# Block means of the first batch's values: from vector reductions to products with a constant matrix

## The chip, the cores and the metric

The kernel runs on one core of a Trainium2 chip. Its engines have queues of their own, each in a fixed order: TensorE (PE, with its weight loads as PEld), VectorE (DVE), ScalarE (ACT), GpSimd (POOL), and SyncE (SP), which issues nearly all transfers. What is measured is the device time of one execution in microseconds (us); lower is better. Line numbers such as L349 are lines of the kernel before; where the changed kernel's own lines are meant, the text says so.

## The reference

Three stages follow each other: an attention, a feed-forward block h - tanh(h), and a gated feed-forward block with a norm in front.

```python
block, window = (32, 16)                     # B, H, S, D = 2, 8, 768, 64; nb = 24
k_sum = k.reshape(B, H, nb, block, D).max(axis=3)
v_sum = v.reshape(B, H, nb, block, D).mean(axis=3)
scores_l = scale * q @ k^T                   # kept only where |i - j| < 16
scores_s = scale * q @ k_sum^T + log(block)
a = softmax(concat(scores_l, scores_s))
x = a @ concat(v, v_sum)                     # 1536 tokens x 512
h = x @ w_in;  x = (h - tanh(h)) @ w_out     # 512 -> 2048 -> 512
xn = x / rms(x) * rms_g
out = (silu(xn @ w_gate) * (xn @ w_val)) @ w_out2
```

What the change touches is `v_sum` of batch 0 (24 blocks by 512 columns), and, lightly, `k_sum`.

## The kernel before, in words

**Attention.** A tile is 128 queries of one batch, 6 tiles a batch. A unit u is half the heads of one tile: u = 0 to 11 belong to batch 0, 12 to 23 to batch 1; the units of batch 0 are taken in the order 0, 2, 1, 3, 4, 5, ... For a unit, `scores` (L333) multiplies the queries with a window of keys beside the 24 block maxima on TensorE, four products of 120 columns (L346); VectorE adds the mask and finds the maximum (L349, four steps of two instructions); ScalarE takes the exponential (L351); VectorE finishes the sums (L352, L353); GpSimd scales (L354). `trans` (L357) turns the result on TensorE (L361) and copies it (L366), and `pv` (L369) multiplies it with the values (L378), after which ScalarE writes the high part of a tile's output x (L381) and VectorE its low part (L382). Three tiles make a group; the first product of the feed-forward block with group 0, `up_step` (L405, products L395 to L397), needs the x of units 0 to 5. "The third x" below is the one of units 4 and 5.

**Block maxima and means.** `ksum_a` (L248) loads one of two halves of a batch's keys for one parity of heads and reduces them on VectorE (L263 to L266); `ksum_b` (L268) turns them into a table (L272, L274 to L276). `vsum_a` (L278) loads a quarter of the values, laid out with a block's 32 rows side by side, and sums them: in batch 0 three quarters by a reduction on VectorE (L294), one by five additions on GpSimd (L290, L292). `vsum_b` (L296) turns the sums with four transposes (L300) and writes them, scaled, into a values tile (L304 on ScalarE, L306 on VectorE), from which a second tile gets them by two small transfers (L331).

**Weights.** Each of 16 + 16 weight tiles of the first block arrives as pairs of 32-bit words; ScalarE and VectorE make one float of each pair (L162 to L165), and ScalarE or VectorE and GpSimd split it into two parts (L170 or L172, L173). The first words of `w_in` are worked on while the attention of batch 0 runs.

**What sets the order.** `task` (L580) gives every piece of work a due time; pieces are emitted in that order, and a list scheduler with a time model of its own then lays the instructions of each engine into a fixed queue. An engine that stands at an instruction whose input is late stands still. `tc.issue_after(i)` ties what is emitted under it behind instruction i of the same engine. SP issues its transfers in order; at most eight are under way, since the ninth waits for the first.

Of the kernel before, what the change touches and what calls it, by code (L numbers as in the profile page):

```python
# [2 lines left out]

# [50 lines left out]
TP1 = 1.0  # L54
TC = 0.6
TK01 = 1
TV = 4
TK1 = -8
TV1 = -8
TD0 = 11  # L60
# [17 lines left out]
TVL = (6, 16)
ORD = [0, 2, 1, 3]
TKB = (4, 6)  # L80
VE = ((0, 1, 0, 0), (1, 1, 1, 1))
DTV = 0.25
TVS = 10
TCKW = {"schedule_with_timeline_sim": True}


# [1 line left out]
def attn_moe_kernel(ctx: ExitStack, tc: tile.TileContext, ins, out, dbg=None):  # L88
    nc = tc.nc
    V, A, G, T = nc.vector, nc.scalar, nc.gpsimd, nc.tensor  # L90

    cst = ctx.enter_context(tc.tile_pool(name="cst", bufs=1))
    wp = ctx.enter_context(tc.tile_pool(name="wp", bufs=SLOTS_A))
# [9 lines left out]
    ps_t = att_ctx.enter_context(tc.tile_pool(name="ps_t", bufs=PST, space=PSUM))  # L103
    ap1 = att_ctx.enter_context(tc.tile_pool(name="ap1", bufs=1))
# [6 lines left out]
    state = {}  # L111

    def f(ap):
        return ap.bitcast(F32)

    sel = cst.tile([128, 256], F32, name="sel")
    ident = sel[:, 64:192]
    rg = cst.tile([128, KD], F32, name="rg")
    mask = ap1.tile([128, 3, WID], F32, name="mask")


    def consts():
        nc.sync.dma_start(out=mask, in_=ins["mask"])
        nc.sync.dma_start(out=rg, in_=ins["rms_g"])


    jobs = []
# [120 lines left out]
    def ksum_a(b, par, hf):  # L248
        if not kwin:
            for h2 in range(2):  # L250
                for p2 in range(2):
                    kwin[0, p2, h2] = kp_.tile([128, KT, 4 * WID], F32, name="kw")
        if b:
            kwin[b, par, hf] = kp_.tile([128, KT, 4 * WID], F32, name="kw")
        kw = kwin[b, par, hf]
        m1 = ap2.tile([128, KT, 2, 4], F32, name="m1")
        m2 = ap2.tile([128, KT, 2, 4], F32, name="m2")
        if not hf:
            kmax[b, par] = ap2.tile([128, 4, TPB, 2], F32, name="mx")
        ts = slice(hf * KT, hf * KT + KT)  # L260
        nc.sync.dma_start(out=kw[:, :, 0:4 * LOC], in_=ins["kw"][b, par, :, ts])
        w = kw[:, :, 0:4 * LOC].rearrange("p t (j k c) -> p t j k c", j=4, k=4)
        V.tensor_reduce(m1.rearrange("p t j k -> p t (j k)"), kw[:, :, 96:288].rearrange("p t (x c) -> p t x c", c=24), AX.X, ALU.max)  # L263
        for j in range(2):
            V.tensor_reduce(m2[:, :, j], w[:, :, 3 * j, :, 16:24], AX.X, ALU.max)
        V.tensor_tensor(kmax[b, par][:, :, ts].rearrange("p k t j -> p t j k"), m1, m2, ALU.max)  # L266
# [11 lines left out]
    def vsum_a(b, c, pool, name):  # L278
# [3 lines left out]
        raw = pool.tile([128, 1024], U32, name=name) if name == "raw" else pool.tile([128, 2, 512], F32R, name=name).rearrange("p a n -> p (a n)")  # L282
        rr = f(raw)[:, 0:S]
        nc.sync.dma_start(out=rr, in_=ins["vt"][b, c])
        r = rr.rearrange("p (n j) -> p n j", j=BLK)
        o = vt_[b][:, c, LOC:]
        if VE[b][c]:
            n = BLK // 2
            while n > 1:
                G.tensor_tensor(r[:, :, 0:n], r[:, :, 0:n], r[:, :, n:2 * n], ALU.add)  # L290
                n //= 2
            G.tensor_tensor(o, r[:, :, 0], r[:, :, 1], ALU.add)  # L292
        else:
            V.tensor_reduce(o, r, AX.X, ALU.add)  # L294

    def vsum_b(b):  # L296
        vt = vt_.pop(b)
        ps = ps_t.tile([128, 512], F32, name="t")
        for c in range(4):
            T.transpose(ps[0:WID, c * 128:(c + 1) * 128], vt[:, c], ident)  # L300
        if b == 0:
            v_of[0] = 0
            vsum[b] = v_b[0][LOC:WID, 0]
            A.activation(v_b[0][LOC:WID, 0], ps[LOC:WID], AF.Copy, scale=1.0 / BLK)  # L304
            if PVS[b]:
                V.tensor_scalar(v_b[0][LOC:WID, 1], ps[LOC:WID], 1.0 / BLK, None, ALU.mult)  # L306
            else:
                A.activation(v_b[0][LOC:WID, 1], ps[LOC:WID], AF.Copy, scale=1.0 / BLK)
            return
        vsum[b] = ap1.tile([128, DM], F32, name="vsum")[LOC:WID]  # L310
        if PVS[b]:
            V.tensor_scalar(vsum[b], ps[LOC:WID], 1.0 / BLK, None, ALU.mult)
        else:
            A.activation(vsum[b], ps[LOC:WID], AF.Copy, scale=1.0 / BLK)
# [72 lines left out]
    for j, nch in enumerate(NCH):  # L387
# [4 lines left out]
    acc, part, gs, last = {}, {}, {}, {}  # L392
# [187 lines left out]
    def task(key, at, fn, *req):  # L580
        plan[key] = (at + SHIFT.get(key, 0), len(plan), fn, req)
# [14 lines left out]
    for par in range(2):  # L596
        at = TK01 * par
        for hf in range(2):
            task(f"ka0{par}{hf}", at + hf / 4, lambda par=par, hf=hf: ksum_a(0, par, hf))
        task(f"kb0{par}", TKB[par], lambda par=par: ksum_b(0, par), f"ka0{par}0", f"ka0{par}1", "sel")  # L600
    for c in range(4):
        task(f"va0{c}", TV + c * DTV, lambda c=c: vsum_a(0, c, wp, "w"))
    task("vs0", TV * 0 + TVS, lambda: vsum_b(0), "sel", *[f"va0{c}" for c in range(4)])
    at = t_sc(2 * TPB)
    for par in range(2):
        for hf in range(2):
            i = 2 * par + hf + 4 - KBUF
            task(f"ka1{par}{hf}", at + TK1 + 4 * par + 2 * hf, lambda par=par, hf=hf: ksum_a(1, par, hf), *([f"sc{[4, 5, 10, 11][i]}"] if i >= 0 else []))
        task(f"kb1{par}", at - 2 + par, lambda par=par: ksum_b(1, par), f"ka1{par}0", f"ka1{par}1")
    for c in range(4):  # L610
        task(f"va1{c}", at + TV1 + 3 * c, lambda c=c: vsum_a(1, c, rawp, "raw"))
# [18 lines left out]
    at = TM0  # L630
# [62 lines left out]
    for i in range(n0, len(steps) + LAG):  # L693
# [18 lines left out]
        j, g, m, first, end = steps[i - LAG]  # L712
# [5 lines left out]
        if j == len(NCH) - 1 and end:  # L718
            t = free["t"]
# [31 lines left out]
        down2(*prev, j)  # L751


_INS = ["q", "kw", "vt", "vw", "mask", "sel", "rms_g", "w_in", "w_out", "w_gate", "w_val", "w_out2"]


def layouts(q, k, v, moe_w_in, moe_w_out, moe2_w_gate, moe2_w_val, moe2_w_out, moe2_rms_g):
# [15 lines left out]
    vt = v.transpose(0, 2, 1, 3).reshape(B, S, DM)  # L773
# [17 lines left out]
    return {  # L791
        "q": qz.reshape(B, TPB, 128, 1024),
        "kw": np.ascontiguousarray(kw).reshape(B, 2, 128, TPB, 4 * LOC),
        "vt": np.ascontiguousarray(vs), "vw": np.ascontiguousarray(vw),
        "mask": mask,
        "sel": np.eye(128, dtype=np.float32).reshape(128, 2, 1, 64).repeat(2, axis=2).reshape(128, 256),
        "rms_g": np.ascontiguousarray(moe2_rms_g.reshape(KD, 128).T),
# [21 lines left out]
```

## Time and profile before

| | |
|---|---|
| median of 3 runs | 659.62 us (656.51, 659.62, 776.9) |
| profiled execution, its own time | 658.16 us |
| its span in the trace | 656.4 us |
| TensorE busy | 625.1 us (95%) |
| VectorE busy | 451.1 us (69%) |
| ScalarE, GpSimd busy | 324.6 us (49%), 227.7 us (35%) |
| share of TensorE in the chain that ended last | 86% (VectorE 9%) |

From about 82 us on TensorE is busy nearly all the time, but for some 8 us around 357 us and 360 to 380 us, between the two feed-forward blocks, and the last few. In the first 50 us it stands still for 18 us. The granted clock is read with care there: products of the same form take twice as long at 16 us as at 22 us, and the clock column shows 1.00 for both.

### The profile page before, as it was taken

The numbers are of one execution on the slowest core, as the hardware profiler recorded it, in microseconds if no ns is written. First come the engines' busy times: TensorE is split into PE (matmuls) and PEld (weight loads), VectorE is DVE, ScalarE is ACT, GpSimd is POOL, SyncE is SP. The second block draws the span as 40 slices with busy tenths as digits, with TensorE's granted clock in tenths as the row PEclk, the third lists the DMA queues.
The fourth block names the chain that finished last, engine by engine and source line by source line (L and its number), as shares of the span: only waits on it lengthen the run. The fifth ranks groups of instructions, "written<-read, shape, count | busy, mean of one in ns | idle before, by whom it ended". The sixth has DMA issues, their size and how long they took to land.

```text
span 656.4 us, 9788 instructions
## 1 busy us (share of the span) xinstructions
PE 625.1 (95%) x3576; PEld 571.3 (87%) x3576; DVE 451.1 (69%) x979; ACT 324.6 (49%) x783; POOL 227.7 (35%) x237
## 2 busy tenths in 40 slices
PE   3779999999999999999997799999999999999997
PEld 3768898899998999999996699999999999999995
DVE  5898654368887666756469476766768767678644
ACT  2776676445444444444556584454544554454320
POOL 1467621112322222440014020635634644555300
PEclk9888999999999999999999789999999999999999
DMA  9986321212322322111000000121121211111013
GB/s 335 353 280 205 120 93 43 89 65 97 128 97 86 107 93 101 65 65 65 0 33 32 33 1 0 65 82 47 65 91 38 96 66 64 65 66 64 1 49 144
DMA packets 19641, 58.91 MB, mean 90 GB/s; under 512 B 2169, under 2 KB 5497, under 8 KB 19593
## 3 DMA queue, kind: packets, MB, share of 16 engines
q1 hardware_dynamic: 19592, 58.29, 25.7%
q8 instruction: 28, 0.46, 0.3%
q14 instruction: 21, 0.16, 0.1%
HBM read 54.84 MB, written 3.15 MB: 88 GB/s over the span
## 4 chain that ended last, share of the span: by engine, by line
PE 86%; DVE 9%; ACT 2%; issue 1%; DMA 1%; POOL 0%; SPq 0%; DVEq 0%; ACTq 0%
PE h L395 8%; PE h L397 8%; PE h L396 8%; PE acc L401 6%; PE acc L402 6%; PE acc L403 6%; PE t L401 5%; PE t L402 5%; PE t L403 5%; PE acc L395 4%; PE acc L397 4%; PE acc L396 4%; PE accx L397 3%; PE accx L396 3%; PE accx L395 3%; PE t L346 2%
## 5 line engine op out<-in xcount | busy, mean ns | idle before, releaser
L173 POOL TENSOR_TENSOR w<-dt,w 128x512 fp32r<-128x512 f32 (+1 forms) x59 | 73.8, 1252 | 191.6 <-ACT w L170 139.8
L395 PE MATMUL h<-x,w 128*128 128x384 f32 x248 | 85.5, 345 | 7.5 <-DVE s L414 6.4
L397 PE MATMUL h<-x,w 128*128 128x384 f32 x248 | 84.7, 343 | 2.3 <-DVE x L382 2.3
L162 ACT ACTIVATE da<-raw 128x512 f32<-128x512 f32 x68 | 45.6, 670 | 81.5 <-DMA raw<-w_out 32.3
L396 PE MATMUL h<-x,w 128*128 128x384 f32 x248 | 84.6, 341 | 0.0
L414 DVE TENSOR_TENSOR s<-h,s 128x384 f32<-128x384 f32 x64 | 35.5, 555 | 46.5 <-ACT s L413 46.2
L417 DVE TENSOR_TENSOR g<-s,g 128x384 fp32r<-128x384 f32 x64 | 47.5, 743 | 22.4 <-ACT g L416 22.2
L395 PE MATMUL acc<-x,w 128*128 128x384 f32 x168 | 57.8, 344 | 0.0
L396 PE MATMUL acc<-x,w 128*128 128x384 f32 x168 | 57.3, 341 | 0.0
L402 PE MATMUL acc<-w,g 128*128 128x512 f32 x144 | 57.2, 397 | 0.0
L402 PE MATMUL t<-w,g 128*128 128x512 f32 x144 | 56.8, 395 | 0.0
L403 PE MATMUL t<-w,g 128*128 128x512 f32 x144 | 56.6, 393 | 0.0
L437 DVE TENSOR_TENSOR part<-t,part 128x512 f32<-128x512 f32 x60 | 40.5, 686 | 23.2 <-PE t L403 23.2
L395 PEld LDWEIGHTS h<-x,w 128*128 128x128 f32 x248 | 47.3, 191 | 10.5 <-DVE s L414 6.8
L403 PE MATMUL acc<-w,g 128*128 128x512 f32 x144 | 56.1, 397 | 0.0
L397 PE MATMUL acc<-x,w 128*128 128x384 f32 x168 | 55.7, 341 | 0.0
L401 PE MATMUL acc<-w,g 128*128 128x512 f32 x144 | 55.3, 400 | 0.0
L401 PE MATMUL t<-w,g 128*128 128x512 f32 x144 | 54.8, 394 | 0.3 <-DVE part L437 0.3
L164 DVE SCALAR_TENSOR_TENSOR dt<-da,dt 128x512 uint32<-128x512 uint32 x68 | 53.8, 791 | 1.6
L165 DVE SCALAR_TENSOR_TENSOR dt<-raw,dt 128x512 uint32<-128x512 uint32 x68 | 51.4, 756 | 1.3
L170 ACT ACTIVATE w<-dt 128x512 fp32r<-128x512 f32 (+1 forms) x55 | 32.0, 583 | 40.7 <-DVE dt L165 40.2
L413 ACT ACTIVATE s<-h 128x384 f32<-128x384 f32 x64 | 30.9, 483 | 41.2 <-PE h L397 41.0
(130 smaller groups left out, 1547.4 us busy)
## 6 DMA issues: line engine op xcount, KB each, us to landing
raw<-w_out SPq DMA_DIRECT2D x28, 512.0 KB, 3.2
raw<-w_in SPq DMA_DIRECT2D x16, 512.0 KB, 3.9
q<-q SPq DMA_DIRECT2D x12, 512.0 KB, 7.9
raw<-w_gate SPq DMA_DIRECT2D x12, 512.0 KB, 3.2
raw<-w_val SPq DMA_DIRECT2D x12, 512.0 KB, 3.3
kw<-kw SPq DMA_DIRECT2D x8, 576.0 KB, 6.0
v<-vw SPq DMA_DIRECT2D x12, 384.0 KB, 4.6
out_dram<-part SPq DMA_DIRECT2D x12, 256.0 KB, 2.0
```

The costliest lines, as they stand in the source:

```text
L162: A.activation(a, r[:, :, 1].bitcast(F32), AF.Copy, scale=2.0 ** -112)
L164: V.scalar_tensor_tensor(t, a.bitcast(U32), 3, t, ALU.logical_shift_left, ALU.bitwise_or)
L165: V.scalar_tensor_tensor(t, r[:, :, 1], 0x80000000, t, ALU.bitwise_and, ALU.bitwise_or)
L173: G.tensor_tensor(lo, d, f(hi), ALU.subtract)
L395: T.matmul(o, wh, xh, start=start, stop=False, **kw)
L396: T.matmul(o, wl, xh, start=False, stop=False, **kw)
L397: last["PE"] = T.matmul(o, wh, xl, start=False, stop=stop, **kw)
L401: T.matmul(o, g[:, 0, js], w[:, 0], start=first, stop=False)
L402: T.matmul(o, g[:, 1, js], w[:, 0], start=False, stop=False)
L403: last["PE"] = T.matmul(o, g[:, 0, js], w[:, 1], start=False, stop=end)
L417: last["DVE"] = V.tensor_tensor(gg[:, 1], t, f(gg[:, 0]), ALU.subtract)
L437: V.tensor_tensor(part[t], a, part[t], ALU.add)
```

## The change

For batch 0 the values now come in their own row order, 128 rows by 512 columns, two such tiles to a transfer and three transfers (`vn`), in place of four (`vt`). A constant `mean` matrix (128 by 130, entries 1/32) is loaded, and six products of 128 rows by 512 columns, summed in place in one bank, give the 24 block means at once at the rows where they are wanted. The reductions on VectorE, the additions on GpSimd and the four transposes of batch 0 are gone; the two copies into the values tile stay, without the scale. Batch 1 keeps its additions on GpSimd.

Beside that, the second half of the first keys is issued from ScalarE's queue instead of SP's; the norm's scales `rg` are loaded later; the maxima of batch 1 are tied behind the last score step emitted so far (`last["SC"]`); and due times change, so that the value loads are issued ahead of the second and third query tiles.

```diff
-TV = 4
+TV = 1.5
-TSEL = 0.3
-TQ = (0.2, 3)
-TVL = (6, 16)
+TSEL = 0.15
+TQ = (0.4, 3)
+TVL = (2.6, 16)
-VE = ((0, 1, 0, 0), (1, 1, 1, 1))
-TVS = 10
+TVS = 8
+    mean = ap1.tile([128, WID + 2 * (TPB - 1)], F32, name="mean")
     def consts():
         nc.sync.dma_start(out=mask, in_=ins["mask"])
-        nc.sync.dma_start(out=rg, in_=ins["rms_g"])
...
-        nc.sync.dma_start(out=kw[:, :, 0:4 * LOC], in_=ins["kw"][b, par, :, ts])
+        (nc.scalar if not (b or par) and hf else nc.sync).dma_start(out=kw[:, :, 0:4 * LOC], in_=ins["kw"][b, par, :, ts])
...
+        with tc.issue_after(last["SC"].ins) if b else nullcontext():
+            V.tensor_reduce(m1.rearrange("p t j k -> p t (j k)"), kw[:, :, 96:288].rearrange("p t (x c) -> p t x c", c=24), AX.X, ALU.max)
...
+    def vsum_a(b, c):
+        if b == 0:
+            vn[c] = wp.tile([128, 2, 512], F32R, name="w")
+            nc.sync.dma_start(out=f(vn[c]), in_=ins["vn"][c])
+            return
...
-            V.tensor_reduce(o, r, AX.X, ALU.add)
...
     def vsum_b(b):
+        ps = ps_t.tile([128, 512], F32, name="t")
+        if b == 0:
+            for t in range(TPB):
+                T.matmul(ps[0:WID], mean[:, 2 * (TPB - 1 - t):2 * (TPB - 1 - t) + WID], f(vn[t // 2])[:, t % 2], start=(t == 0), stop=(t == TPB - 1))
+            v_of[0] = 0
+            vsum[b] = v_b[0][LOC:WID, 0]
+            A.activation(v_b[0][LOC:WID, 0], ps[LOC:WID], AF.Copy)
+            V.tensor_copy(v_b[0][LOC:WID, 1], ps[LOC:WID])
+            return
...
-                V.tensor_tensor_reduce(P[:, k], ps[:, i * WID:(i + 1) * WID], mk, -0.125, 3e38, ALU.add, ALU.min, nb[:, k:k + 1])
+                last["SC"] = V.tensor_tensor_reduce(P[:, k], ps[:, i * WID:(i + 1) * WID], mk, -0.125, 3e38, ALU.add, ALU.min, nb[:, k:k + 1])
...
+    task("mean", TV - 0.1, lambda: nc.sync.dma_start(out=mean, in_=ins["mean"]))
+    task("rg", 20, lambda: nc.sync.dma_start(out=rg, in_=ins["rms_g"]))
+    task("vs0", TVS, lambda: vsum_b(0), "mean", *[f"va0{c}" for c in range(3)])
+    mean = np.zeros((128, WID + 2 * (TPB - 1)), np.float32)
+    mean[np.arange(128), LOC + 2 * (TPB - 1) + 2 * TPB * (np.arange(128) // 64) + np.arange(128) // BLK % 2] = 1.0 / BLK
```

**How instructions move.** SP's queue from its first transfer, before (`kw` keys, `q0` to `q2` query tiles, `vt` values, `vw` windows of values, `raw` weight words):

```order
L261 DMA kw_121<-kw 128x3x384
L318 DMA q0_112<-q 128x1024
L261 DMA kw_123<-kw 128x3x384
...
L261 DMA kw_124<-kw 128x3x384
L318 DMA q1_113<-q 128x1024
L284 DMA w_168<-vt 128x768
...
L323 DMA v0_115<-vw 96x1024
L318 DMA q2_114<-q 128x1024
L156 DMA raw_238<-w_in 128x1024
```

and in the change (its own line numbers; `kw_124`, the second half of the first keys, is the first thing in ScalarE's queue instead):

```order
L259 DMA kw_122<-kw 128x3x384
L590 DMA sel_109<-sel 128x256
L314 DMA q0_113<-q 128x1024
...
L599 DMA mean_112<-mean 128x130
L282 DMA w_160<-vn 128x1024
...
L319 DMA v0_116<-vw 96x1024
L314 DMA q1_114<-q 128x1024
L314 DMA q2_115<-q 128x1024
L154 DMA raw_229<-w_in 128x1024
```

The second query tile now stands behind all values and the first window of values; the first weight words stand, as before, behind the third query tile.

TensorE's queue from its first product, before (`mx` maxima, `t_160` and `t_184` the two key tables, `h_` score products, `P_` the turned units, `acc` the first product with values):

```order
L272 MATMUL t_160<-mx_127,sel_109 128x48 x2
L346 MATMUL h_193<-kw_121,q0_112 128x120 x2
L346 MATMUL h_198<-kw_121,q0_112 128x120 x2
L346 MATMUL h_215<-kw_121,q1_113 128x120 x4
L272 MATMUL t_184<-mx_146,sel_109 128x48 x2
L300 MATMUL t_231<-sel_109,vt0_166 120x128
L346 MATMUL h_259<-kw_122,q0_112 128x120 x2
L346 MATMUL h_264<-kw_122,q0_112 128x120 x2
L361 MATMUL t_249<-sel_109,P_190 120x128 x4
L346 MATMUL h_298<-kw_122,q1_113 128x120 x4
```

and in the change:

```order
L271 MATMUL t_168<-mx_128,sel_109 128x48 x2
L342 MATMUL h_183<-kw_122,q0_113 128x120 x2
L342 MATMUL h_188<-kw_122,q0_113 128x120 x2
L271 MATMUL t_174<-mx_146,sel_109 128x48 x2
L300 MATMUL t_200<-w_160,mean_112 120x512 x2
L357 MATMUL t_240<-sel_109,P_180 120x128 x4
L300 MATMUL t_200<-w_162,mean_112 120x512 x2
L300 MATMUL t_200<-w_164,mean_112 120x512 x2
L342 MATMUL h_213<-kw_122,q1_114 128x120 x4
L342 MATMUL h_250<-kw_123,q0_113 128x120 x2
```

All six products with the values stand ahead of the scores of unit 2 (`h_215` before, `h_213` now), which were fourth in the queue.

VectorE's queue after the maxima of the last half of batch 0's keys, before (`sm_192` sums of unit 0, `P_212` scores of unit 2):

```order
L266 TENSOR_TENSOR mx_146<-m1_152,m2_153 128x6x4
L352 TENSOR_SCALAR sm_192<-sm_192 128x4
L294 TENSOR_REDUCE vt0_166<-w_168 128x24
L353 RECIPROCAL sm_192<-sm_192 128x4
L349 ISA P_212,nb_213<-h_215,mask_111 128x120
L349 ISA nb_213 128x1
...
L274 COPY kw_122<-t_184 128x96
```

and in the change (`dt` weight words, `P_210` scores of unit 2):

```order
L265 TENSOR_TENSOR mx_146<-m1_152,m2_153 128x6x4
L349 RECIPROCAL sm_182<-sm_182 128x4
L273 COPY kw_123<-t_174 128x96
L161 TENSOR_SCALAR dt_232<-raw_229 128x512
L162 SCALAR_TENSOR_TENSOR dt_232<-da_231,dt_232 128x512
L163 SCALAR_TENSOR_TENSOR dt_232<-raw_229,dt_232 128x512
L161 TENSOR_SCALAR dt_271<-raw_268 128x512
L304 COPY v0_116<-t_200 24x512
L345 ISA P_210,nb_211<-h_213,mask_111 128x120
L345 ISA nb_211 128x1
```

The work on the first weight tile, and the start of the second's, now stand ahead of unit 2's scores; before, the scores of units 2, 1 and 3 stood ahead of it. Up to the third x VectorE's queue holds 38 score steps (42 before), 8, 7 and 7 instructions of the three kinds on weight words (6, 6 and 5 before), one reduction of batch 1's maxima (two before), one sum step less and none of the three reductions of values. From the second half of batch 0's attention on, TensorE's queue is the same in both up to the second feed-forward block, but for a few neighbours that change places.

## Rows read from the trace of the kernel before

**Rows 1.** Busy time by stretch: stretch, length, then us (count) per engine, granted clock, DMA.
```profile
sum 50.30, PE 31.95 PEld 28.52 DVE 40.73 ACT 28.68 POOL 21.40; mean PE 7.99 PEld 7.13 DVE 10.18 ACT 7.17 POOL 5.35
...
49.20:65.60 16.40, 15.36 (x80) 14.57 (x80) 14.73 (x42) 9.95 (x29) 12.58 (x15) 0.90 0.61 206
65.60:82.00 16.40, 15.82 (x157) 14.18 (x156) 10.96 (x47) 10.69 (x40) 11.13 (x18) 1.00 0.38 120
```
**Rows 2.** Waits of TensorE, whole span: who waited for whom, total, times, longest.
```profile
PE h L397 <- DVE x L382: 2.3, 1, 2.3
```
**Rows 3.** Chain that ended last, 0 to 60 us: start, length, work.
```profile
49.61 0.59 DVE x L382
50.24 0.54 PE h L397
```
**Rows 4.** Groups on VectorE, 0 to 60 us: busy us, mean ns, idle before.
```profile
L349 DVE CUSTOM_DVE_ANT_0 P<-h,mask 128x120 f32<-128x120 f32 x32 | 7.2, 272 | 0.1
L165 DVE SCALAR_TENSOR_TENSOR dt<-raw,dt 128x512 uint32<-128x512 uint32 x7 | 6.8, 965 | 0.0
L163 DVE TENSOR_SCALAR dt<-raw 128x512 uint32<-128x512 uint32 x7 | 5.4, 767 | 0.0
L263 DVE TENSOR_REDUCE m<-kw 128x24 f32<-128x576 f32 x7 | 5.2, 741 | 4.5 <-DMA kw<-kw 4.5
L164 DVE SCALAR_TENSOR_TENSOR dt<-da,dt 128x512 uint32<-128x512 uint32 x7 | 5.0, 717 | 0.2
L265 DVE TENSOR_REDUCE m<-kw 128x12 f32<-128x96 f32 x14 | 2.9, 240 | 0.0
L294 DVE TENSOR_REDUCE vt<-w 128x24 f32<-128x768 f32 x3 | 2.8, 943 | 0.0
L281 DVE MEMSET vt<- 128x384 f32 x2 | 0.8, 378 | 0.9 <-PEq L809 0.9
L274 DVE COPY kw<-t 128x96 f32<-128x96 f32 x3 | 0.8, 251 | 1.2 <-PE t L272 1.2
L306 DVE TENSOR_SCALAR v<-t 24x512 f32<-24x512 f32 x1 | 0.7, 699 | 0.0
```
**Rows 5.** Timeline of VectorE: start, us, instruction, idle before and releaser.
```profile
4.61 0.75 DVE L263 TENSOR_REDUCE m<-kw 128x24 f32<-128x576 f32 x1 [2.94 <-DMA kw<-kw]
...
7.48 0.75 DVE L263 TENSOR_REDUCE m<-kw 128x24 f32<-128x576 f32 x1 [1.56 <-DMA kw<-kw]
```
**Rows 6.** Stretches again; the last two columns are the DMA share and GB/s.
```profile
0.00:5.00 5.00, 0.00 (x0) 0.00 (x0) 1.14 (x3) 1.28 (x1) 0.20 (x4) 1.00 0.61 213
5.00:8.00 3.00, 0.00 (x0) 0.00 (x0) 1.41 (x5) 0.00 (x0) 0.00 (x0) 1.00 1.00 359
8.00:16.00 8.00, 6.15 (x25) 5.44 (x25) 6.05 (x33) 2.28 (x11) 1.82 (x4) 1.00 1.05 398
16.00:20.00 4.00, 3.75 (x18) 3.57 (x19) 3.17 (x15) 2.42 (x13) 3.37 (x6) 1.00 1.03 337
20.00:22.00 2.00, 2.00 (x21) 2.00 (x20) 1.21 (x11) 1.57 (x6) 1.10 (x3) 1.00 1.06 404
```
**Rows 7.** Timeline of TensorE (start, us): 32-bit products at 16 us and at 341 us.
```profile
16.25 2.06 PE L346 MATMUL h<-kw,q 128*128 128x120 f32 x8 [0.25 <-DVE kw L274]
...
340.72 1.50 PE L475 MATMUL t<-s,part 128*128 128x128 f32 x12
341.98 0.42 PE L395 MATMUL h<-x,w 128*128 128x384 f32 x1
```
**Rows 8.** Timeline of VectorE: second table's copy; two steps on words, GpSimd standing.
```profile
15.94 0.25 DVE L274 COPY kw<-t 128x96 f32<-128x96 f32 x1
...
24.18 0.42 DVE L163 TENSOR_SCALAR dt<-raw 128x512 uint32<-128x512 uint32 x1
24.52 0.68 DVE L165 SCALAR_TENSOR_TENSOR dt<-raw,dt 128x512 uint32<-128x512 uint32 x1
```
**Rows 9.** Timeline of TensorE: one tile's products with the values.
```profile
42.02 1.15 PE L378 MATMUL acc<-pt,v 120*64 120x64 f32 x32
```

More of the change, by code (lines that the diff above doesn't have):

```diff
@@ L1 @@
 import heapq
-from contextlib import ExitStack
+from contextlib import ExitStack, nullcontext
 import concourse.bass as bass
@@ L68 @@
 KBUF = 4
-PVS = (1, 1)
 PB = 4
@@ L110, in attn_moe_kernel @@
     rawp = att_ctx.enter_context(tc.tile_pool(name="rawp", bufs=RB))
-    state = {}
+    state, last = {}, {}
     def f(ap):
@@ L260, in ksum_a @@
         ts = slice(hf * KT, hf * KT + KT)
-        nc.sync.dma_start(out=kw[:, :, 0:4 * LOC], in_=ins["kw"][b, par, :, ts])
+        (nc.scalar if not (b or par) and hf else nc.sync).dma_start(out=kw[:, :, 0:4 * LOC], in_=ins["kw"][b, par, :, ts])
         w = kw[:, :, 0:4 * LOC].rearrange("p t (j k c) -> p t j k c", j=4, k=4)
[L263 to L266, printed above, removed]
+        with tc.issue_after(last["SC"].ins) if b else nullcontext():
+            V.tensor_reduce(m1.rearrange("p t j k -> p t (j k)"), kw[:, :, 96:288].rearrange("p t (x c) -> p t x c", c=24), AX.X, ALU.max)
+            for j in range(2):
+                V.tensor_reduce(m2[:, :, j], w[:, :, 3 * j, :, 16:24], AX.X, ALU.max)
+            V.tensor_tensor(kmax[b, par][:, :, ts].rearrange("p k t j -> p t j k"), m1, m2, ALU.max)
     def ksum_b(b, par):
@@ L276, in ksum_b @@
         G.tensor_copy(sm2, sm[:, 0:1].to_broadcast([128, KT, 96]))
-    def vsum_a(b, c, pool, name):
+    vn = {}
+    def vsum_a(b, c):
[3 more added lines that the diff above has]
+            return
         if c == 0:
@@ L281, in vsum_a @@
             V.memset(vt_[b][:, :, 0:LOC], 0.0)
-        raw = pool.tile([128, 1024], U32, name=name) if name == "raw" else pool.tile([128, 2, 512], F32R, name=name).rearrange("p a n -> p (a n)")
-        rr = f(raw)[:, 0:S]
-        nc.sync.dma_start(out=rr, in_=ins["vt"][b, c])
+        rr = f(rawp.tile([128, 1024], U32, name="raw"))[:, 0:S]
+        nc.sync.dma_start(out=rr, in_=ins["vt"][c])
         r = rr.rearrange("p (n j) -> p n j", j=BLK)
[L286 to L293, printed above, removed]
-            V.tensor_reduce(o, r, AX.X, ALU.add)
@@ L296, in vsum_b @@
-    def vsum_b(b):
+        n = BLK // 2
+        while n > 1:
+            G.tensor_tensor(r[:, :, 0:n], r[:, :, 0:n], r[:, :, n:2 * n], ALU.add)
+            n //= 2
+        G.tensor_tensor(vt_[b][:, c, LOC:], r[:, :, 0], r[:, :, 1], ALU.add)
+    def vsum_b(b):
+        ps = ps_t.tile([128, 512], F32, name="t")
[7 more added lines that the diff above has]
+            return
@@ L297, in vsum_b @@
         vt = vt_.pop(b)
-        ps = ps_t.tile([128, 512], F32, name="t")
         for c in range(4):
             T.transpose(ps[0:WID, c * 128:(c + 1) * 128], vt[:, c], ident)
[L301 to L309, printed above, removed]
@@ L310, in vsum_b @@
         vsum[b] = ap1.tile([128, DM], F32, name="vsum")[LOC:WID]
[L311 to L314, printed above, removed]
+        V.tensor_scalar(vsum[b], ps[LOC:WID], 1.0 / BLK, None, ALU.mult)
     def qload(i):
@@ L391, in attn_moe_kernel @@
         m0 += nch
-    acc, part, gs, last = {}, {}, {}, {}
+    acc, part, gs = {}, {}, {}
     def triple(o, wh, wl, xh, xl, start, stop, **kw):
@@ L598, in attn_moe_kernel @@
         for hf in range(2):
-            task(f"ka0{par}{hf}", at + hf / 4, lambda par=par, hf=hf: ksum_a(0, par, hf))
+            task(f"ka0{par}{hf}", at + hf / 10, lambda par=par, hf=hf: ksum_a(0, par, hf))
         task(f"kb0{par}", TKB[par], lambda par=par: ksum_b(0, par), f"ka0{par}0", f"ka0{par}1", "sel")
-    for c in range(4):
-        task(f"va0{c}", TV + c * DTV, lambda c=c: vsum_a(0, c, wp, "w"))
-    task("vs0", TV * 0 + TVS, lambda: vsum_b(0), "sel", *[f"va0{c}" for c in range(4)])
+    for c in range(3):
+        task(f"va0{c}", TV + c * DTV, lambda c=c: vsum_a(0, c))
+    task("mean", TV - 0.1, lambda: nc.sync.dma_start(out=mean, in_=ins["mean"]))
+    task("rg", 20, lambda: nc.sync.dma_start(out=rg, in_=ins["rms_g"]))
+    task("vs0", TVS, lambda: vsum_b(0), "mean", *[f"va0{c}" for c in range(3)])
     at = t_sc(2 * TPB)
@@ L610, in attn_moe_kernel @@
     for c in range(4):
-        task(f"va1{c}", at + TV1 + 3 * c, lambda c=c: vsum_a(1, c, rawp, "raw"))
+        task(f"va1{c}", at + TV1 + 3 * c, lambda c=c: vsum_a(1, c))
     task("vs1", at + TV1 + 14, lambda: vsum_b(1), *[f"va1{c}" for c in range(4)])
@@ L751, in attn_moe_kernel @@
         down2(*prev, j)
-_INS = ["q", "kw", "vt", "vw", "mask", "sel", "rms_g", "w_in", "w_out", "w_gate", "w_val", "w_out2"]
+_INS = ["q", "kw", "vn", "vt", "vw", "mean", "mask", "sel", "rms_g", "w_in", "w_out", "w_gate", "w_val", "w_out2"]
 def layouts(q, k, v, moe_w_in, moe_w_out, moe2_w_gate, moe2_w_val, moe2_w_out, moe2_rms_g):
@@ L793, in layouts @@
         "kw": np.ascontiguousarray(kw).reshape(B, 2, 128, TPB, 4 * LOC),
-        "vt": np.ascontiguousarray(vs), "vw": np.ascontiguousarray(vw),
+        "vt": np.ascontiguousarray(vs[1]), "vn": np.ascontiguousarray(vt[0].reshape(TPB // 2, 2, 128, DM).transpose(0, 2, 1, 3)),
+        "mean": mean, "vw": np.ascontiguousarray(vw),
         "mask": mask,
```

## The prediction, made before the changed kernel ran

> **What bounds the kernel now.** From about 50 us to the end TensorE is the bound: in the two stretches behind 49.2 us it stands still for 1.04 and 0.58 us [rows 1]. The change touches nothing behind that but small exchanges in the queues, so what it is worth is read from the first 50 us, where TensorE is busy for 31.95 of 50.30 us and the other engines decide when its dense work starts.
>
> Who decides is seen in two views. Among TensorE's waits stands one of 2.3 us for the low part of x, a VectorE step [rows 2], and the chain of waits shows its end: that step starts at 49.61 us and the product behind it at 50.24 us [rows 3]. This is the third x. VectorE is busy for 40.73 of those 50.30 us [rows 1], so it stood still for 9.6 us, nearly all of it early: it waits for the keys [rows 5] and the first table. I therefore add up the head along VectorE's queue: the work ahead of the third x, and the time in which the queue stands.
>
> **The work on VectorE.** Removed: three reductions of values, 3 x 0.943 = 2.83 us, and one memset, 0.38 us [rows 4]. The memset ran while VectorE waited for keys, and the same wait covers its place now, so it is worth nothing. The tie moves one reduction of batch 1's maxima behind the third x: 0.741 + 2 x 0.240 = 1.22 us. Four score steps fewer stand ahead of it; a step is 7.2 / 32 = 0.225 us, together 0.90 us. Against that the new queue has more word steps ahead of the third x: two of L163, one of L164, two of L165, 2 x 0.767 + 0.717 + 2 x 0.965 = 4.18 us by the means [rows 4]. Those means hold the slowing that is seen while GpSimd works; the first word steps now run while GpSimd has nothing to do, where two of the kinds took 0.42 and 0.68 us [rows 8] and not 0.767 and 0.965. For two of the one and one of the other that is 1.0 us less. The copy of the means (L306, 0.70 us) stays. So the work falls from 40.73 to 40.73 - 0.38 - 2.83 - 1.22 - 0.90 + 4.18 - 1.0 = 38.6 us.
>
> **The time in which VectorE stands.** *Keys.* The halves were reduced from 4.61 and 7.48 us on [rows 5]; each reduction is some 1.3 us, so the first table's maxima ended at 8.8 us. Now the second half does not stand behind the query tile. If both halves share the engines evenly, both land when 1.18 MB are in: 5 us x 213 GB/s = 1.07 MB by 5 us and 0.11 MB more at 359 GB/s [rows 6], 5.3 us, and 0.7 us more until the reduction starts (1.70 MB were in at 6.8 us by the same rows, and the second reduction started at 7.48 us). Two reductions from 6.0 us end at 8.7 us. If they do not share, the first lands at 4.6 us and the maxima end at 7.4 us. The gain lies between 0.1 and 1.4 us; I take 0.4, near the even share, since the engines are full from 5 us on (share 1.00 in [rows 6]).
>
> The Trainium skill (DMA: Bandwidth & Descriptors, section "Issuing engines are not separate DMA queues") says that transfers from different engines run on the same 16 DMA engines and interleave, so that a second issuer saves only its issue time. By that rule the gain is the 0.1 us of the even share, and the sum below 0.3 us higher; no run here shows it yet.
>
> *First weight words.* With the maxima 0.4 us earlier, unit 0's scores and the second table follow about as before; that table's copy ended at 16.2 us [rows 8], so VectorE now comes to the first weight words at 15.8 us. These are behind four key halves, selector, three query tiles, mask, mean matrix, values and a value window: 6.80 MB with themselves. The rows of bytes [rows 6] give 1.07, 2.15, 5.33 and 6.68 MB at 5, 8, 16 and 20 us, so 6.80 MB at 20.3 us; with 0.7 us the words can be used at 21.0 us, the second tile's (7.33 MB) at 22.3 us. VectorE stands for 5.2 us. Before, reductions of values and the scores of two units filled that time; unit 2's scores are now queued behind the waiting step, and behind them its exponentials, its scaling and its turn.
>
> *Products.* A 32-bit product is two instructions. Twelve of 128 columns took 341.98 - 340.72 = 1.26 us, 0.105 each, at the upper of TensorE's two levels (1.2 and 2.4 GHz) [rows 7]; scaled by columns, one of 512 is 0.42 us there and 0.84 us at the lower level. Eight score instructions took 2.06 us at 16.25 us, 0.26 each, so TensorE was at the lower level although it had worked since 10 us. The first two products start near 15.4 us, 0.4 us and the copy and one transpose ahead of where unit 1's scores stood at 16.25 us [rows 7]. I take their four instructions at the lower level (3.4 us), four transposes like score instructions (1.0 us) and the remaining eight at the upper (3.4 us): they end at 23.2 us, unit 2's scores 1.0 us later, and VectorE starts on those at 24.4 us. The values themselves are in by then (4.84 MB, 15.5 us) and so is the second query tile (5.76 MB, 18.0 us): neither is waited for, and the removed transposes and additions on GpSimd (21.40 us busy of 50.30 [rows 1]) lay beside other work and are worth nothing.
>
> The price of these products has no row. Below, it is bounded by a cost that does not grow with columns (12 x 0.105 = 1.3 us: then the words decide, and unit 2 starts 0.5 us earlier); above, by the score instructions scaled by columns at the lower level, 0.26 x 512 / 120 = 1.1 us each, 13.2 us in all: 7.2 us later. I scale the rows of 128 columns, which are nearest in kind.
>
> **The sum.** By 24.4 us VectorE has done: memset 0.38, four reductions of keys 4.9, unit 0's scores 0.9, two table copies 0.5, its small steps 0.3, words 2.2, the copy 0.7, in all 9.9 us. The other 28.7 us follow without a wait that I can name, so the third x ends at 53.1 us, 2.8 us later than 50.3 us. Before, TensorE used its wait for the third x for the next tile's products with the values, 1.15 us [rows 9]; these stand behind it now and are still to do. Of the 0.58 us that TensorE stands still from 65.6 us on, I let the word steps done early win back 0.3. Together +2.8 + 1.15 - 0.3 = +3.6 us. Against the profiled execution of 658.16 us that is **661.8 us**; the median of the runs shown is 1.5 us above that execution.
>
> **Rivals.** *The work counts, the standing does not* (faster). If VectorE's late start were made good, because the words done early free it where it is nearly full (14.73 of 16.40 us from 49.2 us on [rows 1]), the removed 2.83 us and the tied 1.22 us would remain: 654.1 us. For it: the queue is full from 24 us on, and 4.2 us of later work is done ahead. Against it: TensorE, not VectorE, is the bound behind 50 us. It decides where TensorE's first dense product starts below 47 us.
>
> *The products stay at the lower level* (slower than forecast). If all twelve instructions run at 0.84 us, they end 3.3 us later, unit 2's scores take 2.1 us for 1.0, and everything behind follows 4.2 us later: 666 us; with 1.1 us each, 669 us. For it: TensorE was at the lower level at 16 us, and its stops between unit 0 and the second table are longer now. Against it: the products themselves keep it busy without a gap. It decides where unit 2's first score step comes after 27 us.
>
> *Nothing happens.* If the early words repay just what the wait costs, the time is 658 us.
>
> **Numbers.** The forecast has 0.50, the slower rival 0.17, the faster one 0.20, no change 0.13. The range, 654 to 668 us, reaches from the faster rival to the middle of the slower one's prices and takes in the bounds of the key gain and of the products; the forecast's own is 659 to 665 us. A difference of 2% is 13 us, about what a measurement of this kernel can tell from no change. No case but the dearest end of the slower rival comes near it: same 0.96, slower 0.03, faster 0.01.
>
> **What would show it.** VectorE standing for about 5 us ahead of its first step on weight words near 21 us; no score step of unit 2 before 23 us (they stood ahead of the copy at 15.94 us [rows 8]); the product instructions at some 0.84 us and then 0.42 us; the third x ending near 53 us; TensorE's idle time behind that unchanged. The prediction is wrong if the first words are in before 18 us, if TensorE's dense work starts no later than 50 us, or if the stop around 357 us between the two feed-forward blocks changes by more than 2 us, which I hold for untouched since the queues there are the same.

## The result and the profile after

The changed kernel takes 665.93 us (median of 665.4, 665.93 and 666.85; a fourth run, 784 us at a mean granted clock of 0.755, is left out; with it the median is 666.39 us). Its ratio to the kernel before, run beside it, is 1.0121 [1.0101, 1.0141], and in a second comparison (e1 below) 1.0129 [1.0108, 1.0150]: slower by 8.0 to 8.5 us, where 3.6 us had been forecast. All comparisons of times below are ratios to the kernel before on the same chip; a ratio is turned into us with the median of that kernel in the same group of runs, 657.4 to 658.5 us.

The profile is that of e1 (the same kernel; the profiled execution took 667.46 us). Its line numbers are a few below those of before: L300 is the products, L304 the copy of the means, L342 and L345 the scores on TensorE and VectorE, L161 to L163 the word steps, L374 the products with the values, L378 the low part of x, L391 to L393 the first dense products. The busy time of the two parts of the head, columns as in [rows 1]:

```profile
0.00:24.50 24.50, 13.01 (x46) 8.31 (x46) 9.62 (x34) 5.55 (x13) 2.62 (x9) 1.00 0.95 334
24.50:58.10 33.60, 22.92 (x194) 20.01 (x194) 31.74 (x114) 23.36 (x85) 23.95 (x22) 0.80 0.80 264
```

VectorE does 9.62 us of work before unit 2's scores and 31.74 of the 33.6 us behind them. Its timeline, and TensorE's, at the place where the queue was expected to stand:

```profile
14.96 0.26 DVE L273 COPY kw<-t 128x96 f32<-128x96 f32 x1 [1.11 <-PE t L271]
21.29 0.43 DVE L161 TENSOR_SCALAR dt<-raw 128x512 uint32<-128x512 uint32 x1 [6.08 <-DMA raw<-w_in]
...
23.79 0.70 DVE L304 COPY v<-t 24x512 f32<-24x512 f32 x1
24.52 0.28 DVE L345 CUSTOM_DVE_ANT_0 P<-h,mask 128x120 f32<-128x120 f32 x1
```

```profile
14.72 3.51 PE L300 MATMUL t<-w,mean 128*120 128x512 f32 x4
18.07 0.60 PE L357 MATMUL t<-sel,P 128*120 128x128 f32 x4
18.50 3.60 PE L300 MATMUL t<-w,mean 128*120 128x512 f32 x8
21.94 1.49 PE L342 MATMUL h<-kw,q 128*128 128x120 f32 x12
```

VectorE stands for 6.08 us ahead of the first words, with unit 2's scores queued behind them at 24.52 us; TensorE meanwhile does the products, 0.88 us an instruction at first and 0.45 us then. The end of the head, from the chain of waits (start, length, work), answers to [rows 3]:

```profile
49.80 1.37 DVE dt L163
...
51.16 0.02 SPq L154
...
51.23 5.07 DMA raw<-w_out
...
56.39 0.43 DVE dt L161
...
57.49 0.61 DVE x L378
...
58.15 0.44 PE h L393
```

The third x ends at 58.10 us, where it ended at 50.20 [rows 3]: 7.9 us later. Just ahead of it stands a step on words of `w_out` whose load was issued at 51.2 us, as soon as a word step had ended which, as the chain has it, freed one of the three raw buffers; the load took 5.07 us. With 1.15 us for the next tile's products with the values, which now stand behind the third x (at 63.41 us), this makes 9.05 us; the two profiled executions differ by 9.3 us. From 58.15 to 75 us TensorE does not stand still, and its two stops between the feed-forward blocks are 6.4 and 2.4 us, before 6.4 and 2.0. So nearly all of the loss is made ahead of the dense product that needs the third x.

### The profile page after: what moved, and what is told of

Read it like the earlier page. It is cut to its first block, busy times and chain, and to the rows that moved or that the text cites. A ratio compares the mean times of both kernels' runs of the same rounds, so it can differ in the third digit from the quotient of the medians.

```text
span 782.1 us, 9810 instructions
## 1 busy us (share of the span) xinstructions
PE 754.0 (96%) x3584; PEld 620.7 (79%) x3584; DVE 456.2 (58%) x975; ACT 330.9 (42%) x783; POOL 220.9 (28%) x232
## 4 chain that ended last, share of the span: by engine, by line
PE 89%; DVE 7%; DMA 1%; ACT 1%; issue 1%; SPq 0%; DVEq 0%
PE h L393 9%; PE h L391 9%; PE h L392 9%; PE acc L397 6%; PE acc L398 6%; PE acc L399 6%; PE t L397 5%; PE t L399 5%; PE t L398 5%; PE acc L393 4%; PE acc L392 4%; PE acc L391 4%; PE accx L391 3%; PE accx L393 3%; PE accx L392 3%; PE t L342 2%
## 5 line engine op out<-in xcount | busy, mean ns | idle before, releaser
L171 POOL TENSOR_TENSOR w<-dt,w 128x512 fp32r<-128x512 f32 (+1 forms) x59 | 72.1, 1223 | 244.5 <-ACT w L168 178.8
L391 PE MATMUL h<-x,w 128*128 128x384 f32 x248 | 96.2, 388 | 2.8 <-DVE s L410 2.7
L393 PE MATMUL h<-x,w 128*128 128x384 f32 x248 | 95.2, 385 | 0.8 <-DVE x L378 0.8
L392 PE MATMUL h<-x,w 128*128 128x384 f32 x248 | 95.4, 385 | 0.0
L398 PE MATMUL acc<-w,g 128*128 128x512 f32 x144 | 66.3, 460 | 0.0
L399 PE MATMUL t<-w,g 128*128 128x512 f32 x144 | 65.8, 457 | 0.0
L398 PE MATMUL t<-w,g 128*128 128x512 f32 x144 | 65.7, 456 | 0.0
L399 PE MATMUL acc<-w,g 128*128 128x512 f32 x144 | 64.8, 456 | 0.0
L391 PE MATMUL acc<-x,w 128*128 128x384 f32 x168 | 64.7, 386 | 0.0
L393 PE MATMUL acc<-x,w 128*128 128x384 f32 x168 | 64.7, 385 | 0.0
L392 PE MATMUL acc<-x,w 128*128 128x384 f32 x168 | 64.6, 385 | 0.0
L397 PE MATMUL t<-w,g 128*128 128x512 f32 x144 | 63.7, 457 | 0.2 <-DVE part L433 0.2
L397 PE MATMUL acc<-w,g 128*128 128x512 f32 x144 | 63.8, 458 | 0.0
L413 DVE TENSOR_TENSOR g<-s,g 128x384 fp32r<-128x384 f32 x64 | 44.9, 702 | 22.8 <-ACT g L412 22.7
L391 PEld LDWEIGHTS h<-x,w 128*128 128x128 f32 x248 | 49.1, 198 | 11.1 <-DVE s L410 3.2
L163 DVE SCALAR_TENSOR_TENSOR dt<-raw,dt 128x512 uint32<-128x512 uint32 x68 | 54.7, 806 | 1.4
L392 PEld LDWEIGHTS h<-x,w 128*128 128x128 f32 x248 | 49.0, 198 | 8.1
```

The costliest lines, as they stand in the source:

```text
L163: V.scalar_tensor_tensor(t, r[:, :, 1], 0x80000000, t, ALU.bitwise_and, ALU.bitwise_or)
L171: G.tensor_tensor(lo, d, f(hi), ALU.subtract)
L392: T.matmul(o, wl, xh, start=False, stop=False, **kw)
L393: last["PE"] = T.matmul(o, wh, xl, start=False, stop=stop, **kw)
L397: T.matmul(o, g[:, 0, js], w[:, 0], start=first, stop=False)
L398: T.matmul(o, g[:, 1, js], w[:, 0], start=False, stop=False)
```

## The experiments

Three theories. **A (order):** loads and queue order make unit 2 late; the products fit in. **B (products):** they cost TensorE's time wherever they stand. **D** (called C in e2's text): the tie or the key load on ScalarE's queue does it. fp32r is a rounded 32-bit type: one of these products is one instruction in it (e12), and two in fp32 (e3). All twelve kernels in one table; "third x" is its end in the profiled execution (50.2 us before).

| kernel | ratio [95%] | us | third x |
|---|---|---|---|
| e1 the change | 1.0129 [1.0108, 1.0150] | +8.5 | 58.1 |
| e2 second query first | 1.0068 [1.0050, 1.0086] | +4.5 | 55.3 |
| e3 due times of before | 1.0054 [1.0038, 1.0070] | +3.6 | 55.1 |
| e4 due times alone | 1.0067 [1.0050, 1.0084] | +4.4 | 53.9 |
| e5 e3, half the products | 1.0006 [0.9994, 1.0017] | +0.4 | 49.2 |
| e6 e3, fp32r, GpSimd's loads | 1.0122 [1.0104, 1.0141] | +8.0 | 55.9 |
| e7 tie and key queue alone | 0.9977 [0.9966, 0.9989] | -1.5 | 48.0 |
| e8 e1, four raw buffers | 1.0079 [1.0051, 1.0106] | +5.2 | 55.8 |
| e9 e6, loads held back | 1.0106 [1.0083, 1.0130] | +7.0 | 56.4 |
| e10 e7, four raw buffers | 1.0032 [1.0019, 1.0045] | +2.1 | 52.3 |
| e11 e3, four raw buffers | 1.0050 [1.0034, 1.0065] | +3.3 | 55.3 |
| e12 e3, fp32r, ScalarE rounds | 0.9947 [0.9930, 0.9964] | -3.5 | 47.9 |

The third x tells the sign in all but e5, which ties, and the size within 2.5 us: the place was the right one to look at. One caution holds for all: the planner lays the queues anew for every edit, so a difference between two kernels is never the edit alone, and what is believed below is believed where a row shows it.

**e1**, the change again.

> The changed kernel as it is, for a profile to be read beside the others of this group: 6 to 9 us above the kernel before. Theory A (order): unit 2's score steps stand on VectorE behind the block means, the first weight words and the wait for the second query tile, the third x ends at 55 to 58 us instead of 49.6, with a wait of VectorE for a load of w_out's words just ahead of it. Theory B (the products): the block means' matmuls cost TensorE and the path some 8 us of the head wherever they stand; the wait for the words is not on the path.

As theory A had it; the wait for the words of `w_out` was known from the first profile of the changed kernel, where it was 0.6 us. What follows from it stands above.

**e2**, the second query tile's load ahead of the values.

```diff
-TQ = (0.4, 3)
+TQ = (0.4, 1.3)
```

> The changed kernel with the second query tile's load issued ahead of the values again (one due time changed); products, tie and the key load on ScalarE's queue stay. Theory A (order): unit 2's scores stand ahead of the products and of the first weight words again, the third x ends at 49 to 52 us and the time is within 2 us of the kernel before. Theory B (the products cost wherever they stand): still 5 to 8 us above the kernel before. Theory C (the key load on the other queue or the tie): as B.

+4.5 us: neither A's 2 nor quite B's 5 to 8. One due time gives back 4 of the 8.5 us, and as much stays.

**e3**, all due times as before.

```diff
-TV = 1.5
+TV = 4
-TSEL = 0.15
+TSEL = 0.3
-TQ = (0.4, 3)
-TVL = (2.6, 16)
+TQ = (0.2, 3)
+TVL = (6, 16)
-TVS = 8
+TVS = 10
...
-            task(f"ka0{par}{hf}", at + hf / 10, ...)
+            task(f"ka0{par}{hf}", at + hf / 4, ...)
```

The last pair, the due time of the second half of the keys, belongs to the change too.

> The changed kernel with all due times of the head as in the kernel before: values after the queries, block means later, products kept. Theory A (order): within 2 us of the kernel before, the third x by 52 us. Theory B (the products): 5 to 8 us above it.

+3.6 us, so A alone falls; B's 5 to 8 us are not met either. TensorE's timeline, then the stretch from 16 to 25 us in e3, then in the kernel before, then VectorE's timeline in e3:

```profile
15.45 3.37 PE L300 MATMUL t<-w,mean 128*120 128x512 f32 x4
18.66 0.60 PE L357 MATMUL t<-sel,P 128*120 128x128 f32 x4
19.10 1.88 PE L300 MATMUL t<-w,mean 128*120 128x512 f32 x4
20.82 1.05 PE L342 MATMUL h<-kw,q 128*128 128x120 f32 x8
21.70 1.88 PE L300 MATMUL t<-w,mean 128*120 128x512 f32 x4
...
23.86 1.94 PE L342 MATMUL h<-kw,q 128*128 128x120 f32 x16
```

```profile
16.00:25.00 9.00, 9.00 (x39) 5.20 (x38) 4.31 (x19) 5.36 (x19) 1.72 (x4) 1.00 1.03 345
```

```profile
16.00:25.00 9.00, 7.22 (x47) 6.79 (x47) 7.28 (x37) 6.96 (x27) 4.84 (x9) 1.00 1.03 344
```

```profile
21.01 0.43 DVE L161 TENSOR_SCALAR dt<-raw 128x512 uint32<-128x512 uint32 x1 [3.69 <-DMA raw<-w_in]
21.46 0.28 DVE L345 CUSTOM_DVE_ANT_0 P<-h,mask 128x120 f32<-128x120 f32 x1
```

With the products TensorE is full there (9.00 of 9.00 us) and does fewer instructions, and VectorE, whose work comes through TensorE's scores, does 4.31 us in place of 7.28. VectorE's long wait there is booked to the first weight words, but unit 1's scores, queued right behind them, start on TensorE only at 20.82 us. In e5 VectorE's first step on them comes 0.64 us behind that start (18.79 and 19.43 us), and by this spacing it would come at 21.46 us in e3, which is when it came: not the words held this step up, but the full TensorE. VectorE was relieved in a stretch where it then had to wait for the engine that took the work over.

**e4**, the kernel before with e1's due times: e3's diff read the other way.

> The kernel before, its block means by sums on VectorE and GpSimd, with the changed due times alone: values loaded ahead of the second and third query tiles. Theory A (order) splits: if the load order alone makes it, 4 us or more above the kernel before, with unit 2's first score step later than 22 us; if it takes the products between, within 2 us. Theory B (the products): within 1 us of the kernel before.

+4.4 us without any of the products. TensorE's timeline shows why, VectorE's what it does:

```profile
16.66 1.11 PE L361 MATMUL t<-sel,P 128*120 128x128 f32 x4
20.04 2.91 PE L346 MATMUL h<-kw,q 128*128 128x120 f32 x12 [2.27 <-DMA q<-q]
```

```profile
22.14 0.28 DVE L349 CUSTOM_DVE_ANT_0 P<-h,mask 128x120 f32<-128x120 f32 x1 [3.78 <-PE h L346]
```

The second query tile, behind the values, is in at 20 us; unit 2's first score step is at 22.14 us. In e1 a wait for it up to 20 us lies under the products, which end at 22.1 us.

**e7**, tie and key load alone, on the kernel before.

```diff
-        nc.sync.dma_start(out=kw[:, :, 0:4 * LOC], ...)
+        (nc.scalar if not (b or par) and hf else nc.sync).dma_start(...)
...
+        with tc.issue_after(last["SC"].ins) if b else nullcontext():
```

> The kernel before with two parts of the change alone: the later block maxima tied, and the second key load of the first parity on ScalarE's queue. Theory B: within 1 us of the kernel before. Theory D: 2 to 4 us above it.

-1.5 us, a little better than before: D falls. In size the parts now add up: tie and queue -1.5 (e7), products at the old due times 3.6 + 1.5 = 5.1 (e3 against e7, with all that goes with them: the values' layout and loads, the sums gone, `rg` later), due times 4.4 (e4), in all +8.0 for the +8.5 measured. That they add up is not shown to be more than arithmetic: each was measured in a queue order of its own, and in e1 the wait for the second query tile lies under the products.

**e5**, three of the six products left out.

```diff
-            for t in range(TPB):
+            for t in range(0, TPB, 2):
...
```

> The changed kernel with the due times of before (as e3, which took 3.5 us more than the kernel before) and 3 of the 6 products left out, so that the block means miss every second tile of 128 keys. Theory B (the products occupy TensorE in a stretch where it has no idle time): some 2 to 3 us of TensorE fall away between 14 and 25 us, the score steps behind them move forward by as much and the time comes to within 1.5 us of the kernel before. Theory D (the tie or the key load on ScalarE's queue makes e3's loss): still 3 to 4 us above it.

+0.4 us: 3.2 us less than e3. The product instructions are half, unit 1's score products start at 18.79 us for 20.82 in e3, and those behind all the products 2.9 us earlier (20.97 us, in e3 23.86). VectorE's row shows that its wait now ends with unit 1's scores; the planner has put them ahead of the first words, which e3 has the other way round:

```profile
15.54 2.03 PE L300 MATMUL t<-w,mean 128*120 128x512 f32 x2
...
17.93 1.02 PE L300 MATMUL t<-w,mean 128*120 128x512 f32 x2
18.79 1.05 PE L342 MATMUL h<-kw,q 128*128 128x120 f32 x8
19.67 1.02 PE L300 MATMUL t<-w,mean 128*120 128x512 f32 x2
...
20.97 1.94 PE L342 MATMUL h<-kw,q 128*128 128x120 f32 x16
```

```profile
19.43 0.28 DVE L345 CUSTOM_DVE_ANT_0 P<-h,mask 128x120 f32<-128x120 f32 x1 [2.02 <-PE h L342]
```

**e6**, products in fp32r (values and matrix rounded while they are loaded, from GpSimd's queue).

```diff
-            nc.sync.dma_start(out=f(vn[c]), in_=ins["vn"][c])
+            nc.gpsimd.dma_start(out=vn[c], in_=ins["vn"][c])
...
-  T.matmul(ps[0:WID], mean[...], f(vn[t // 2])[:, t % 2], ...)
+  T.matmul(ps[0:WID], mean[...], vn[t // 2][:, t % 2], ...)
...
```

> As e3, with the values and the constant matrix rounded to fp32r by loads from GpSimd's queue, and all 6 products in fp32r. Theory B: if an fp32r product of 512 columns takes a fraction of the 0.85 us of an fp32 one, the products take under 2 us and the time is within 1 us of the kernel before, or below it. Theory D: 3 to 4 us above it. If the loads from GpSimd's queue arrive late, the products' start shows it (later than 14 us).

+8.0 us, and no test of B: the loads were issued at 1.98 us, beside those of the keys, and the last keys came late (GpSimd's and VectorE's timelines; e3 reduces these keys at 12.27 us):

```profile
1.98 1.60 POOL L282 DMA_DIRECT2D w<-vn  x3
```

```profile
15.89 0.75 DVE L262 TENSOR_REDUCE m<-kw 128x24 f32<-128x576 f32 x1 [0.20 <-DMA kw<-kw]
```

**e9**, the same loads tied behind GpSimd's copies of the first table.

```diff
+            with tc.issue_after(last["KB"].ins):
+                G.dma_start(out=vn[c], in_=ins["vn"][c])
...
```

> As e6 (all 6 products in fp32r, due times of before), with the loads of the values and of the matrix from GpSimd's queue issued behind its copies of the first table, so that they no longer run beside the key loads. Theory B (the fp32 products' TensorE time makes e3's 3.5 us): the second keys are there by 12 us again, the products take under 3 us, and the time is within 1.5 us of the kernel before. If it stays 6 us or more above it, e6's loss was not the early loads, and theory B is in doubt: e5's missing half would have won its 3 us in another way.

+7.0 us. Again the transfers decide: from 16 to 25 us the DMA share is 1.15, a load of weights issued at 10.1 us is used at 26.2 us, and the first product starts at 25.27 us, for 15.45 in e3. What the rounding on the way in adds to that, beside the place of the loads, no run separates. By its own words this left B in doubt, and a kernel with the loads of e3 was needed.

**e12**, loads as in e3, ScalarE rounds.

```diff
-            nc.sync.dma_start(out=f(vn[c]), in_=ins["vn"][c])
+            nc.sync.dma_start(out=vf, in_=ins["vn"][c])
+            A.activation(vn[c], vf, AF.Copy)
...
```

> e3 with all 6 products in fp32r and the loads left where e3 has them (SP's queue, same order): ScalarE rounds the three value tiles and the matrix into fp32r tiles, three steps of 128x1024 more on it. Theory B (the fp32 products' TensorE time makes e3's loss): the products take under 3 us of TensorE in place of e3's 7.1, the first x comes 3 us or more before e3's 40.5 us, and the time is within 1.5 us of the kernel before, or below it. If it stays 3 us or more above, e5's gain was not the TensorE time but the order that came with it.

-3.5 us, the best of all. As in e6 and e9 the values enter the block means rounded to fp32r. TensorE's timeline, the group of the products in e12 and in e3 (busy, mean ns), and what ScalarE pays:

```profile
15.17 1.19 PE L307 MATMUL t<-w,mean 128*120 128x512 f32 x2
...
17.95 0.70 PE L307 MATMUL t<-w,mean 128*120 128x512 f32 x2
...
18.84 0.70 PE L307 MATMUL t<-w,mean 128*120 128x512 f32 x2
19.38 1.94 PE L349 MATMUL h<-kw,q 128*128 128x120 f32 x16
```

```profile
L307 PE MATMUL t<-w,mean 128*120 128x512 f32 x6 | 2.6, 520 | 0.0
```

```profile
L300 PE MATMUL t<-w,mean 128*120 128x512 f32 x12 | 7.1, 728 | 0.0
```

```profile
13.90 1.06 ACT L289 ACTIVATE w<-vf 128x1024 fp32r<-128x1024 f32 x1 [0.67 <-DMA vf<-vn]
...
16.54 1.99 ACT L289 ACTIVATE w<-vf 128x1024 fp32r<-128x1024 f32 x2
```

4.5 us less of TensorE (7.1 to 2.6) put the same score products at 19.38 us instead of 23.86, and the kernel 7 us below e3, although ScalarE works 3.05 us more on the values. With e5 this bears out B for this half of the loss. TensorE's time is not isolated by it, though: the 7 us are more than the 4.5 saved, and as in e5 the planner put the first words behind unit 1's scores, in e3 ahead of them. How the gain divides between the two was not tried, nor were the cheap products with e1's due times.

**e8, e11, e10**, four raw buffers in place of three, on e1, e3 and e7.

```diff
-RB = 3
+RB = 4
```

> The changed kernel with four buffers in place of three for the raw weight words. Theory A: the wait of VectorE for a load of w_out's words ahead of the third x (1.5 us in e1) goes, and 1 to 3 us of the 8.5 us with it. Theory B: no change of the time against e1 (6 to 9 us above the kernel before).

> e3 (the change with the due times of before) with four raw buffers. If the buffers give back only what the changed order lost (theory A): within 1 us of e3, 3 to 4 us above the kernel before. If they give 3 us whatever the order: within 1 us of the kernel before.

> e7 (the kernel before with the tie and the key load on ScalarE's queue) with four raw buffers. Theory A's wait for words is in e7 small (0.5 us of VectorE's waits ahead of the dense stretch): within 1 us of e7, so 0 to 2.5 us below the kernel before. If the buffers give 3 us here too, as in e8, it comes out 4 us below.

e8 is 3.3 us faster than e1 (the intervals do not meet). VectorE's waits from 24.5 to 58.2 us in e8 are one row, and the wait for words is not in it:

```profile
DVE P L345 <- PE t L342: 0.5, 1, 0.5
```

So the buffer was a cost of e1's order. e11 is like e3: with the old due times there was nothing to win. e10 is 3.6 us slower than e7, which nothing had foreseen: more room let the planner issue loads earlier and lay the queues in another way, and TensorE's wait for GpSimd's scaling grew, in e7 and then in e10:

```profile
PE t L362 <- POOL P L355: 5.1, 3, 2.4
```

```profile
PE t L362 <- POOL P L355: 7.8, 4, 3.4
```

What made that order worse is open. It shows that 3 us can come from a new order alone, so e8's 3.3 us are shown as to the wait that went, and as to their size only for this order.

## Why the prediction was right, and where its size was not

The time lies in the range and on the predicted side, but the loss is 8.0 to 8.5 us where 3.6 were forecast, and the time is outside the forecast's own 659 to 665 us. It lies within 1 us of the 666 us that the slower rival named, whose condition the trace denies (unit 2's first score step after 27 us; it came at 24.52). The range takes it in because its upper end was set among that rival's prices: that is luck.

- **The bound, and where to add up:** held. All is decided by the third x, and TensorE's idle time behind it did not change by more than 0.4 us at its two stops. (The sign "dense work starts no later than 50 us" was loosely put: the first products of the dense block, on the earlier x, start at 45.35 us before and at 54.79 us in e1.)
- **Keys, 0.4 us:** held. The first table's products start at 8.43 us, before at 8.84. The first half's reduction now starts at 5.87 us, before at 4.61 [rows 5], and the second follows at once: two queues share the engines, as the Trainium skill (DMA: Bandwidth & Descriptors, "Issuing engines are not separate DMA queues") says. The 0.1 us that I had worked out by its rule was too small.
- **The first words** (21.0 us, standing 5.2 us): 21.29 and 6.08 us. **The products** (3.4, 1.0 and 3.4 us, to 23.2 us): 3.51, 0.4 and 3.60 us, to 22.1 us. So the instructions scaled by columns were priced right, and the rival in which they stay at the lower level falls, as does the faster one. (By the slower rival's own terms, 3.3 us for the products and 1.1 for the scores, its delay is 4.4 us, not 4.2.)
- **Unit 2 at 24.4 us:** 24.52, but not by the forecast's path. There the products and unit 2's scores on TensorE set the date. In e1 the products were done by 22.1 us, and VectorE came to its score step straight from the copy of the means, without a wait: the first words at 21.29 us, the steps on them and the copy set the date. That the two paths end 0.1 us apart is luck.
- **The step that failed:** "The other 28.7 us follow without a wait that I can name, so the third x ends at 53.1 us". They took 33.6 us. 1.86 us of that VectorE stood, 1.5 for the words of `w_out`: a wait made by the change, since two more word tiles ahead of the third x ask for raw buffers that are freed late. e8 takes it away. The other 3.0 us are work: more of VectorE's time than the forecast had carried on. The count of word steps was as forecast (22 for 17), but the small steps, on sums and on maxima, which I let keep their old cost, did not keep it. The groups on VectorE up to the third x, after and before:

```profile
L348 DVE TENSOR_SCALAR sm<-sm 128x4 f32<-128x4 f32 x9 | 5.0, 555 | 0.0
...
L265 DVE TENSOR_TENSOR mx<-m,m 128x24 f32<-128x24 f32 x5 | 2.1, 422 | 0.1
```

```profile
L352 DVE TENSOR_SCALAR sm<-sm 128x4 f32<-128x4 f32 x10 | 4.1, 408 | 2.2 <-ACT P L351 2.2
...
L266 DVE TENSOR_TENSOR mx<-m,m 128x24 f32<-128x24 f32 x6 | 1.2, 196 | 0.1
```

  They take 5.0 + 2.1 us in fewer steps, where the forecast had carried on 4.1 + 1.2: 1.8 of the 3.0 us, an estimate, since the busy times of groups overlap a little. The rest I cannot put to one group. So the term of +2.8 us measured 7.9; +1.15 held (63.41 us), the -0.3 did not show.
- **What the text did not see:** it let the products cost only by unit 2's start. Moving the means to TensorE cost 5.1 us at the old due times (e3 against e7), where TensorE was busy for 7.22 of the 9 us from 16 to 25 us already; e5 and e12 speak for that as the cause. And the changed due times cost 4.4 us without the products (e4). In the forecast both were one date, unit 2's start, so it could not have told which undoing would help: each gives back about half.

## What to carry to other kernels

Before work is moved to an engine, look at that engine's busy time in the stretch where the work will stand, not in the whole span: the engine with 95% was short of work in the head, but not in the 9 us that counted. When a step in a fixed queue becomes late, add the work that follows with the prices it has beside its new neighbours, and ask of each load ahead of the next milestone when its buffer comes free. Where the work has to go there, ask first what its cheapest form costs: here the move paid only after the products had been made 4.5 us cheaper (e12, 3.5 us below the kernel before; 1.5 of these are what tie and key load gave alone in e7).

## What the runs showed of the hardware

**VectorE's small steps beside GpSimd.** The same step (128x4) took 0.16 us or 1.23 us in e1. VectorE's timeline, then GpSimd's:

```profile
32.56 1.23 DVE L348 TENSOR_SCALAR sm<-sm 128x4 f32<-128x4 f32 x1
...
34.31 0.16 DVE L348 TENSOR_SCALAR sm<-sm 128x4 f32<-128x4 f32 x1
```

```profile
32.03 1.73 POOL L171 TENSOR_TENSOR w<-dt,w 128x512 fp32r<-128x512 f32 x1
35.08 1.27 POOL L171 TENSOR_TENSOR w<-dt,w 128x512 fp32r<-128x512 f32 x1 [1.31 <-DVE sm L349]
```

The long one ends with GpSimd's step (33.79 and 33.76 us); the short one lies in GpSimd's pause. Of the nine, the five of 0.16 us lie in pauses of GpSimd, the four of 0.79 to 1.23 us inside its steps. The reductions of keys took 0.74 or 0.75 us throughout. The Trainium skill (SBUF — State Buffer, "Who interferes with whom") says that VectorE and GpSimd share one pair of ports as an exclusive lock, which a `tensor_scalar` can need and a `tensor_reduce` never; the rows agree, and no run here took GpSimd's work away to show it.

**fp32r.** A product of 512 columns was one instruction of 0.35 us in e12 (0.70 for two) at the upper of TensorE's levels, and in fp32 two instructions of 0.45 us in e1. **A third issuer:** 1.6 MB issued from GpSimd's queue at 1.3 to 3.6 us came with a later reduction of the last keys, 15.89 us for 12.27 in e3 (e6): being early in SyncE's queue did not keep the keys ahead of loads issued by another engine.
